# Turns of k between the output halves in pairs 0 to 2, and w2 loaded in thirds

## The chip, the cores and the metric

The kernel runs on one core of a Trainium2 chip. The metric is device time in microseconds (us) of one execution; lower is better. A core has a matrix engine (PE, whose weight loads are shown apart as PEld), a vector engine (DVE), a scalar engine (ACT), a general one (POOL) and SP, which here only issues the transfers (DMAs) from and to the memory outside the core. Each engine works through its own list in order; semaphores hold an instruction back until what it needs is there.

## The reference

A linear attention with decay in blocks, and after it a token-and-channel mixer:

```python
for b in range(nb):                       # 12 blocks of 64 positions
    intra = einsum('bhic,bhjc->bhij', qb, kb) * Dmask
    intra = einsum('bhij,bhjd->bhid', intra, vb)
    inter = einsum('bhid,bhde->bhie', qb * lam_pow, kv_state)
    out[:, :, sl] = intra + inter
    kv_state = lam_block * kv_state + einsum('bhsd,bhse->bhde', kb * rev_pow, vb)
x = out with heads joined                 # 4 x 768 x 512
h = relu(x^T @ w_tok1) @ w_tok2           # over the positions: 768 -> 256 -> 768
u = x + h^T
out = u + relu(u @ w_ch1) @ w_ch2         # over the channels: 512 -> 1536 -> 512
```

q, k, v are 4 x 8 x 768 x 64 in float32. The four weights come in 64-bit floats, read as pairs of 32-bit words.

## The kernel before

**Pairs.** The attention goes over 16 pairs i = 0..15 of two heads of one batch; blocks are 128 positions here, 6 to a pair. Names: `kn`, `qn`, `vn` are k, q, v as loaded; `kT`, `qT` their transposes; `sc` scores, `a` the scores with the decay mask; `kd` k with its decay; `kv` the sums of a block for the state, `sv` the states after the scan over the blocks, `stb` the states as the products need them; `qs` q with its decay; `xT` the outputs of half a pair (three blocks) in PSUM, copied by ACT to `uT`.

**Staging.** One turn of the loop (lines 556 to 619) holds work of three pairs. Turn i writes, in this order: the scores of pair i+1 (`scores`, PE L290, DVE L299) and `scale_q` (POOL L244); the first half of the outputs of pair i (`outputs(i, 0)`, PE L314 and L324, ACT L331); the state of pair i+1 (`state`, PE L257, scan on DVE L265); the second half `outputs(i, 1)`; for pair i+2 the mask scans (DVE L168, pairs 1 to 3 alone) and the turns: `turn_k` (PE L208, ACT L213) in pairs under 8, `turn_q_rows` (PE L228, ACT L229) in pairs under 5, from pair 5 a DVE transpose of q (L218); then `place` (POOL L278, `sv` to `stb`); then, in two halves, `turn_back` of pair i (PE L346 `xp`, ACT L354 `xhi`, DVE L355 `xlo`), with `scale_k` of pair i+2 (`kd`, ACT L237 and POOL L239) between; and last the loads of later pairs. From turn 4 groups of the mixer over positions (`token_hidden` L450, `token_out` L470) are put in.

**Order.** The schedule is by hand: each engine's list is the order in which the code is written.

**Buffers.** The tag "sh" has three PSUM banks, taken in turn by `kt`, `qt`, `kv`, `xp`, `ph`, `pu`; whoever takes a bank waits until the tile three places earlier has been read. `xT` has one bank, so the second half of the outputs waits for ACT's copy (L331) of the first. `kn` and `qn` have two buffers, `vn` three.

**Weights.** w1 comes in three loads (`load_w1`, 512 KB each) at turn -1, w2 in one of 1.5 MB (`load_w2`) at the end of turn 1. `convert_w1(i)` and `convert_w2(i)` put the steps of one third on the list `waiting`: ACT L379, DVE L380, L383, L386, L389, L392, then ACT L374 and POOL L375. `later(n)` writes the next n of them (n+1 where over five wait) between the steps of a turn, so a third that is put on the list at the end of turn i is worked through in turn i+1. In turns 1 to 3 that is w1; its L392 stands on DVE behind both `xlo`, and its L374 on ACT ahead of the next turn's L331.

**After the pairs.** From about 170 us on PE runs the mixer over channels (L645 `ph`, L666 `po`) nearly without a gap to the end.

Of the kernel before, what the change touches and what calls it, by code (L numbers as in the profile page):

```python
# [13 lines left out]
U32 = mybir.dt.uint32  # L14
# [7 lines left out]
def kernel(  # L22
# [23 lines left out]
    nc = tc.nc  # L46
    B, H, S, D = q.shape
# [3 lines left out]
    P = 128  # L51
# [3 lines left out]
    NK = FT // P  # L55
# [23 lines left out]
    def bank(tag, nm, n):  # L79
        return ps.tile([P, n], F32, tag=tag, bufs={"sc": 4, "xT": 1, "sh": 3}[tag], name=nm)  # L80
# [7 lines left out]
    NI = len(pairs)  # L88
# [5 lines left out]
    NKD = 8  # L94
# [71 lines left out]
    def masks(p):  # L166
        for h in (2 * p, 2 * p + 1):
            nc.vector.tensor_tensor_scan(  # L168
                out=mask[:, h],
                data0=lamb[:, h : h + 1].broadcast_to([P, P]),  # L170
                data1=ident,
                initial=0.0,
                op0=ALU.mult,
                op1=ALU.add,
            )
# [12 lines left out]
    n = 1  # L188
    while n < P:
        nc.vector.tensor_mul(  # L190
            out=lamp[:, :, n : 2 * n], in0=lamp[:, :, 0:n], in1=lamp[:, :, n - 1 : n].broadcast_to([P, NP, n])
        )
        n *= 2
    for p in range(NP):
        nc.gpsimd.tensor_copy(
            out=keep[:, p, :, 1:], in_=lamp[:, p, P - 1 : P, None].broadcast_to([P, D, NC - 2])
# [18 lines left out]
    def turn_q(i):  # L215
        qTs[i] = ap.tile([P, S], F32, tag="qT", bufs=2, name=f"qT{i}")
        if i >= NQ:
            nc.vector.transpose(out=qTs[i], in_=loaded[i][1])  # L218
        if i >= NKD:
            kTs[i] = ap.tile([P, S], F32, tag="kT", bufs=2, name=f"kT{i}")  # L220
            nc.vector.transpose(out=kTs[i], in_=krs[i])
# [19 lines left out]
    def scale_q(i):  # L241
        b, p = pairs[i]
        qss[i] = ap.tile([P, NC - 1, P], F32, tag="qs", bufs=2, name=f"qs{i}")
        nc.gpsimd.tensor_mul(  # L244
            out=qss[i],
            in0=qTs[i][:, P:].rearrange("p (c i) -> p c i", i=P),
            in1=lamp[:, p, None, :].broadcast_to([P, NC - 1, P]),
        )

    def state(i):  # L250

        b, p = pairs[i]
        kv = bank("sh", f"kv{i}", D * (NC - 1))
        to = kv.rearrange("p (e c) -> p c e", c=NC - 1)
        for c in range(NC - 1):
            for h in range(2):
                nc.tensor.matmul(  # L257
                    out=to[h * D : (h + 1) * D, c, :],
                    lhsT=kds[i][:, h, c, :],
                    rhs=vns[i][:, h, c, :],  # L260
                    start=(c == 0),
                    stop=(c == NC - 2),
                )
        sv = ap.tile([P, D * (NC - 1)], F32, tag="sv", bufs=1, name=f"sv{i}")
        nc.vector.tensor_tensor_scan(  # L265
            out=sv,
            data0=keep[:, p].rearrange("p e c -> p (e c)"),
            data1=kv,
            initial=0.0,
            op0=ALU.mult,  # L270
            op1=ALU.add,
        )
        st = stb[i % 2]

        def place():
            for h in range(2):
                r = slice(h * D, (h + 1) * D)
                nc.gpsimd.tensor_copy(out=st[r, :, h, :], in_=sv[r].rearrange("p (e c) -> p c e", c=NC - 1))  # L278

        return place  # L280

    def scores(i):
        b, p = pairs[i]
        for g in range(2):
            sc = [bank("sc", f"sc{i}{g}{h}", 3 * P) for h in range(2)]
            for c in range(3):
                cs = slice((3 * g + c) * P, (3 * g + c + 1) * P)
                for h in range(2):
                    r = slice(h * D, (h + 1) * D)
                    nc.tensor.matmul(  # L290
                        out=sc[h][:, c * P : (c + 1) * P],
                        lhsT=kTs[i][r, cs],
                        rhs=qTs[i][r, cs],
                        start=True,
                        stop=True,
                    )
            for h in range(2):
                a = ap.tile([P, 3, P], F32, tag="a", bufs=8, name=f"a{i}{g}{h}")
                nc.vector.tensor_mul(  # L299
                    out=a,  # L300
                    in0=sc[h].rearrange("p (c i) -> p c i", i=P),
                    in1=mask[:, 2 * p + h, None, :].broadcast_to([P, 3, P]),
                )
                weights_of[i, g, h] = a

    def outputs(i, g):
        b, p = pairs[i]
        st = stb[i % 2]
        xT = bank("xT", f"xT{i}{g}", 3 * P)
        for cg in range(3):  # L310
            c = 3 * g + cg
            cs = slice(cg * P, (cg + 1) * P)
            for h in range(2):
                nc.tensor.matmul(  # L314
                    out=xT[h * D : (h + 1) * D, cs],
                    lhsT=vns[i][:, h, c, :],
                    rhs=weights_of[i, g, h][:, cg, :],
                    start=(cg == 0),
                    stop=False,
                )  # L320
            if c == 0:
                continue
            for h in range(2):
                nc.tensor.matmul(  # L324
                    out=xT[h * D : (h + 1) * D, cs],
                    lhsT=st[:, c - 1, h, :],
                    rhs=qss[i][:, c - 1, :],
                    start=False,
                    stop=(cg == 2),
                )  # L330
        nc.scalar.copy(out=uT[b][:, p, 3 * g * P : (3 * g + 3) * P], in_=xT)  # L331
# [68 lines left out]
    def words(b):  # L400
        return uT[b].rearrange("p t s -> p (t s)").bitcast(U32)

    def load_w1(i):
        cs = slice(2 * i, 2 * i + 2)
        nc.sync.dma_start(
            out=words(3).rearrange("p (c f) -> p c f", c=NC)[:, cs],
            in_=w_tok1.bitcast(U32).rearrange("(c s) f -> s c f", s=P)[:, cs],
        )
# [8 lines left out]
            lambda x: x.rearrange("p (c f) -> p c f", f=FT),  # L417
        )

    def load_w2():  # L420
        nc.sync.dma_start(
            out=words(2).rearrange("p (k s) -> p k s", k=NK),
            in_=w_tok2.bitcast(U32).rearrange("(k f) s -> f k s", f=P),
        )

    def convert_w2(i):
        raw = words(2).rearrange("p (n two) -> p n two", two=2)
# [128 lines left out]
    for i in range(-2, NI):  # L556
        if 0 <= i + 1 < NI:
            scores(i + 1)
            scale_q(i + 1)
        if i >= 0:  # L560
            outputs(i, 0)
        place = state(i + 1) if 0 <= i + 1 < NI else None
        work = [groups.popleft() for _ in range(take.get(i, 0))]
        if i == NI - 1:
            work.pop(0)()
        if i >= 0:
            outputs(i, 1)
        if i + 2 < NI:
            turn_q(i + 2)
        if i + 2 < NI:  # L570
            if 0 < i + 2 < NP:
                masks(i + 2)
            turns = [(turn_k, 0), (turn_k, 1)] if i + 2 < NKD else []
            if i + 2 < NQ:
                turns += [(turn_q_rows, 0), (turn_q_rows, 1)]
            if i == -2:
                turns.sort(key=lambda x: x[1])
            for f, g in turns:
                f(i + 2, g)
        if place:  # L580
            place()
        later(1 if work else 2)
        n = early.get(i, len(work) // 4)
        cuts = [0, n, max(n, (3 * len(work) + 1) // 4 if len(work) > 2 else len(work) // 2), len(work)]
        for n in range(3):
            for f in work[cuts[n] : cuts[n + 1]]:
                f()
                later(2 if len(work) < 3 else 1)
            if n < 2 and i >= 0:
                turn_back(i, n)  # L590
                later(1 if work else 2 + n)
            if n == 0 and i + 2 < NI:
                scale_k(i + 2)
        if i == -1:
            load_w1(0)
        if 0 <= i + 3 < NI and i >= -1:
            load_v(i + 3)
        if i == -1:
            load_w1(1)
        if i + 4 < NI:  # L600
            load_kq(i + 4)
        if i == -1:
            load_w1(2)
        if i == 1:
            load_w2()
        if 0 <= i < 3:
            convert_w1(i)
        if 2 <= i < 4:
            convert_w2(i - 2)
        if i == 3:  # L610
            convert_w2(2)
        if i == 5:
            weights[0], load, convert = load_group(0, wa, early_scratch)
        if 5 <= i < 9:
            load(i - 5)
        if 6 <= i < 10:
            convert(i - 6)
        if i == 9:
            waiting.extend(split_block(0, up))
# [153 lines left out]
```

## Time and profile before

| what | value |
|---|---|
| median of 3 runs | 598.8 us (598.21 to 598.8) |
| profiled execution | 597.98 us, of which the span of the instructions is 596.2 us |
| PE busy | 577.9 us (97%) |
| DVE, ACT, POOL busy | 349.7, 155.2, 138.7 us |
| chain that ended last | PE 88%, DMA 4%, DVE 4%, ACT 2%, issue 1% |
| DMA busy | the first ten of 40 slices (149 us) at 9 tenths or more, one of them at 8; then 0 to 2 tenths until shortly before the end |

The span is the time from the first to the last instruction; what lies around it in the profiled execution is 1.78 us. PE is the engine on which nearly all of the time lies, so a stall counts where PE waits, and 18.3 us of the span are all that PE is not busy, start and end included. All of the pairs that the change touches lie in the first 60 us.

### The profile page before, as it was taken

How to read it: one execution, taken by the hardware profiler on the slowest of the kernel's cores; microseconds unless marked ns; L12 is line 12 of the kernel's file. 1: busy time of each engine (PE TensorE's matmuls, PEld its weight loads, DVE VectorE, ACT ScalarE, POOL GpSimd, SP SyncE). 2: the span in 40 equal slices, each digit the busy share in tenths (PEclk: the TensorE clock that was granted, in tenths of full speed). 3: DMA queues.
4: the chain of work that ended last, by engine and by line, in shares of the span. 5: the costliest groups of instructions: out<-in, count | busy, mean ns of one | idle time of the engine just before them, and what ended most of it. 6: DMA issues, size and time to landing. Idle time of an engine off the chain costs nothing.

```text
span 596.2 us, 10673 instructions
## 1 busy us (share of the span) xinstructions
PE 577.9 (97%) x4378; PEld 563.0 (94%) x4378; DVE 349.7 (59%) x663; ACT 155.2 (26%) x322; POOL 138.7 (23%) x131
## 2 busy tenths in 40 slices
PE   5988899999999999999999999999999999999997
PEld 4878798889999999999999999999999999999996
DVE  4797887886633666356533654356533664356664
ACT  3554434343232244112210221112210221101011
POOL 5665532462304367101100010001100010000000
PEclk9999999999999999999999999999999999999999
DMA  9998999999110111012100210012100200016667
GB/s 187 255 227 163 176 167 183 195 155 140 37 37 0 37 50 57 1 36 70 37 1 0 71 50 23 0 36 71 36 1 1 70 1 1 0 24 94 90 89 130
DMA packets 169680, 44.73 MB, mean 75 GB/s; under 512 B 162848, under 2 KB 164000, under 8 KB 169632
## 3 DMA queue, kind: packets, MB, share of 16 engines
q1 hardware_dynamic: 165488, 42.88, 37.4%
q10 hardware_dynamic: 4144, 1.18, 0.9%
q8 instruction: 34, 0.56, 0.4%
q14 instruction: 14, 0.11, 0.1%
HBM read 37.75 MB, written 6.29 MB: 74 GB/s over the span
## 4 chain that ended last, share of the span: by engine, by line
PE 88%; DMA 4%; DVE 4%; ACT 2%; issue 1%; SPq 0%; POOL 0%; DVEq 0%; ACTq 0%
PE ph L645 34%; PE po L666 34%; PE ph L450 6%; DMA kn<-in_k_dram 4%; PE pu L470 4%; PE xT L314 3%; PE sc L290 3%; PE xT L324 2%; PE xp L346 1%; PE kv L257 1%; DVE xlo L355 1%; DVE uT L389 1%; PE kt L208 1%; ACT qT L229 0%; PE qt L228 0%
## 5 line engine op out<-in xcount | busy, mean ns | idle before, releaser
L650 DVE SCALAR_TENSOR_TENSOR hl<-ph,hh 128x384 fp32r<-128x384 f32 x96 | 53.5, 558 | 164.9 <-ACT hh L649 164.9
L666 PE MATMUL po<-hh,c2h 128*128 128x384 f32 x384 | 129.4, 337 | 0.0
L645 PE MATMUL ph<-uh,c1h 128*128 128x384 f32 x384 | 129.2, 337 | 0.0
L645 PE MATMUL ph<-ul,c1h 128*128 128x384 f32 x384 | 129.2, 336 | 0.0
L645 PE MATMUL ph<-uh,c1l 128*128 128x384 f32 x384 | 129.1, 336 | 0.0
L666 PE MATMUL po<-hh,c2l 128*128 128x384 f32 x384 | 128.8, 335 | 0.0
L666 PE MATMUL po<-hl,c2h 128*128 128x384 f32 x384 | 128.6, 335 | 0.0
L649 ACT ACTIVATE hh<-ph 128x384 fp32r<-128x384 f32 x96 | 47.2, 492 | 299.6 <-PE ph L645 297.9
L671 DVE TENSOR_TENSOR uT<-po,uT 128x384 f32<-128x384 f32 x192 | 104.7, 552 | 23.5 <-PE po L666 23.4
L666 PEld LDWEIGHTS po<-hh,c2l 128*128 128x128 f32 x384 | 72.1, 188 | 0.0
L645 PEld LDWEIGHTS ph<-ul,c1h 128*128 128x128 f32 x384 | 72.1, 188 | 0.0
L666 PEld LDWEIGHTS po<-hl,c2h 128*128 128x128 f32 x384 | 72.1, 188 | 0.0
L645 PEld LDWEIGHTS ph<-uh,c1h 128*128 128x128 f32 x384 | 72.1, 188 | 0.0
L645 PEld LDWEIGHTS ph<-uh,c1l 128*128 128x128 f32 x384 | 72.1, 188 | 0.0
L666 PEld LDWEIGHTS po<-hh,c2h 128*128 128x128 f32 x384 | 72.0, 188 | 0.0
L375 POOL TENSOR_TENSOR c1l<-wa,c1h 128x512 fp32r<-128x512 f32 x10 | 12.9, 1290 | 179.9 <-ACT c1h L374 179.9
L535 POOL TENSOR_TENSOR ul<-uT,uh 128x384 fp32r<-128x384 f32 x32 | 36.0, 1154 | 37.5 <-ACT uh L534 37.5
L314 PE MATMUL xT<-a,vn 128*64 128x128 f32 x384 | 36.4, 280 | 1.9 <-ACT uT L331 1.9
L278 POOL COPY stb<-sv 64x320 f32<-64x320 f32 x32 | 26.4, 826 | 43.5 <-DVE sv L265 42.6
L299 DVE TENSOR_TENSOR a<-sc,mask 128x384 f32<-128x384 f32 x64 | 31.2, 550 | 5.7 <-PE sc L290 5.6
L324 PE MATMUL xT<-qs,stb 128*64 128x128 f32 x320 | 31.3, 273 | 0.0
L331 ACT COPY uT<-xT 128x384 f32<-128x384 f32 x32 | 15.3, 478 | 54.4 <-PE xT L324 54.4
(80 smaller groups left out, 758.1 us busy)
## 6 DMA issues: line engine op xcount, KB each, us to landing
raw<-in_moe_w_ch_dram SPq DMA_DIRECT2D x20, 512.0 KB, 3.6
vn<-in_v_dram SPq DMA_DIRECT2D x16, 384.0 KB, 5.5
kn<-in_k_dram SPq DMA_DIRECT2D x30, 192.0 KB, 5.3
out_dram<-y SPq DMA_DIRECT2D x108, 48.0 KB, 1.9
qn<-in_q_dram SPq DMA_DIRECT2D x44, 96.0 KB, 4.2
kr<-in_k_dram SPq DMA_DIRECT2D x32, 96.0 KB, 4.0
uT<-in_moe_w_ch_dram SPq DMA_DIRECT2D x4, 512.0 KB, 4.6
qn<-in_q_dram SPq DMA_DIRECT2D x8, 192.0 KB, 4.4
```

What stands on the lines that cost most here:

```text
L278: nc.gpsimd.tensor_copy(out=st[r, :, h, :], in_=sv[r].rearrange("p (e c) -> p c e", c=NC - 1))
L299: nc.vector.tensor_mul(out=a, in0=sc[h].rearrange("p (c i) -> p c i", i=P), in1=mask[:, 2 * p + h, None, :].broadcast_to([P, 3, P]),)
L314: nc.tensor.matmul(out=xT[h * D : (h + 1) * D, cs], lhsT=vns[i][:, h, c, :], rhs=weights_of[i, g, h][:, cg, :], start=(cg == 0), stop=False,)
L324: nc.tensor.matmul(out=xT[h * D : (h + 1) * D, cs], lhsT=st[:, c - 1, h, :], rhs=qss[i][:, c - 1, :], start=False, stop=(cg == 2),)
L450: nc.tensor.matmul(out=ph, lhsT=w[:, c, fs], rhs=x[:, c], start=(i == 0), stop=(i == 3 * NC - 1))
L470: nc.tensor.matmul(out=pu, lhsT=h[:, kk, cs], rhs=w[:, kk, ss], start=(i == 0), stop=(i == 3 * NK - 1))
L535: nc.gpsimd.tensor_sub(out=ul[:, t], in0=ub[:, t], in1=uh[:, t].bitcast(F32))
L645: nc.tensor.matmul(out=ph, lhsT=w[:, ct, js], rhs=x[:, ct], start=(i == 0), stop=(i == 11))
L649: nc.scalar.activation(hh, ph, AF.Relu)
L650: nc.vector.scalar_tensor_tensor(out=hl, in0=ph, scalar=0.0, in1=hh.bitcast(F32), op0=ALU.max, op1=ALU.subtract)
L666: nc.tensor.matmul(out=po, lhsT=w[:, jj, cs], rhs=h, start=(i == 0), stop=(i == 3 * JG - 1))
L671: nc.vector.tensor_add(out=ub, in0=po, in1=ub)
```

## The change

In turns 0, 1 and 2 the two `turn_k` of pair i+2 move from behind the second half of the outputs to between the halves, and the state of pair i+1 moves from between the halves to behind the second. The other turns are as before. The load of w2 becomes three: the first third in turn 1 ahead of pair 5's k and q, the second (in two pieces, since it crosses from one block of rows to the next) in turn 1 behind them, the last in turn 2 behind pair 5's v and ahead of pair 6's k and q.

```diff
-    def load_w2():
-        nc.sync.dma_start(
-            out=words(2).rearrange("p (k s) -> p k s", k=NK),
-            in_=w_tok2.bitcast(U32).rearrange("(k f) s -> f k s", f=P),
-        )
+    def load_w2(i):
+
+        n = 2 * NK * S // 3
+        k0, k1 = i * n // (2 * S), ((i + 1) * n - 1) // (2 * S)
+        for k in range(k0, k1 + 1):
+            ks = slice(max(i * n, 2 * S * k) - 2 * S * k, min((i + 1) * n, 2 * S * (k + 1)) - 2 * S * k)
+            nc.sync.dma_start(
+                out=words(2).rearrange("p (k s) -> p k s", k=NK)[:, k, ks],
+                in_=w_tok2.bitcast(U32)[k * P : (k + 1) * P, ks],
+            )
...
             outputs(i, 0)
-        place = state(i + 1) if 0 <= i + 1 < NI else None
+        turns = [(turn_k, 0), (turn_k, 1)] if 0 <= i < 3 else []
+        for f, g in turns:
+            f(i + 2, g)
+        place = state(i + 1) if 0 <= i + 1 < NI and not turns else None
...
             outputs(i, 1)
+        if turns:
+            place = state(i + 1)
         if i + 2 < NI:
             turn_q(i + 2)
...
-            turns = [(turn_k, 0), (turn_k, 1)] if i + 2 < NKD else []
+            turns = [(turn_k, 0), (turn_k, 1)] if not turns and i + 2 < NKD else []
...
+        if i in (1, 2):
+            load_w2({1: 0, 2: 2}[i])
         if i + 4 < NI:
             load_kq(i + 4)
...
         if i == 1:
-            load_w2()
+            load_w2(1)
```

PE in turn 1, from the end of the first half of the outputs of pair 1 (`xT_385`) to `turn_back`, before (`kn_236` is k of pair 3, `vn_233` v of pair 2):

```order
L324 MATMUL xT_385<-qs_267,stb_113 64x128 x2
L257 MATMUL kv_397<-vn_233,kd_342 64x64 x10
L314 MATMUL xT_410<-a_263,vn_107 64x128
...
L324 MATMUL xT_410<-qs_267,stb_113 64x128 x2
L208 MATMUL kt_428<-ident,kn_236 128x128 x3
L208 MATMUL kt_433<-ident,kn_236 128x128 x3
L228 MATMUL qt_438<-ident,qn_237 128x128 x3
L228 MATMUL qt_443<-ident,qn_237 128x128 x3
L346 MATMUL xp_453<-ident,uT_60 128x128 x3
```

and the same place now:

```order
L324 MATMUL xT_385<-qs_267,stb_113 64x128 x2
L208 MATMUL kt_398<-ident,kn_236 128x128 x3
L208 MATMUL kt_403<-ident,kn_236 128x128 x3
L314 MATMUL xT_408<-a_263,vn_107 64x128
...
L324 MATMUL xT_408<-qs_267,stb_113 64x128 x2
L257 MATMUL kv_422<-vn_233,kd_342 64x64 x10
L228 MATMUL qt_438<-ident,qn_237 128x128 x3
L228 MATMUL qt_443<-ident,qn_237 128x128 x3
L346 MATMUL xp_453<-ident,uT_60 128x128 x3
```

The turns of k come earlier by a half of the outputs, the sums `kv` later by that half and the turns. In the row of "sh" banks `kv` now stands three places ahead of the first `xp`. The order on DVE and on POOL does not change at all: the scan `sv` still stands directly behind the four `a` and ahead of the mask scans and of the conversion of w1.

ACT at the same place, as a difference:

```order
 L331 COPY uT_60<-xT_385 128x384
-L331 COPY uT_60<-xT_410 128x384
-L213 COPY kT_427<-kt_428 128x384
-L213 COPY kT_427<-kt_433 128x384
-L229 COPY qT_424<-qt_438 128x384
-L229 COPY qT_424<-qt_443 128x384
+L213 COPY kT_397<-kt_398 128x384
+L213 COPY kT_397<-kt_403 128x384
+L331 COPY uT_60<-xT_408 128x384
+L229 COPY qT_435<-qt_438 128x384
+L229 COPY qT_435<-qt_443 128x384
 L379 ACTIVATE uT_61<-uT_63 128x512
```

The two copies of `kT` now stand ahead of the copy of the second half; the steps of the conversion keep their place.

SP, the loads from pair 4's v (`vn_473`) to pair 6's k, before:

```order
L146 DMA vn_473<-in_v_dram 128x12x64
L126 DMA kn_475<-in_k_dram 128x6x64 x2
L104 DMA qn_476<-in_q_dram 32x24x32 x4
L421 DMA uT_62<-in_moe_w_tok_dram 128x2x1536
L146 DMA vn_598<-in_v_dram 128x12x64
L126 DMA kn_600<-in_k_dram 128x6x64 x2
```

and now (w2 is the one into `uT_62`):

```order
L146 DMA vn_473<-in_v_dram 128x12x64
L426 DMA uT_62<-in_moe_w_tok_dram 128x1024
L126 DMA kn_476<-in_k_dram 128x6x64 x2
L104 DMA qn_477<-in_q_dram 32x24x32 x4
L426 DMA uT_62<-in_moe_w_tok_dram 128x512 x2
L146 DMA vn_600<-in_v_dram 128x12x64
L426 DMA uT_62<-in_moe_w_tok_dram 128x1024
L126 DMA kn_603<-in_k_dram 128x6x64 x2
```

A third of w2 moves ahead of pair 5's k and q, and a third behind pair 5's v; pair 6's k still comes behind all of it, and SP issues three DMAs more.

## The prediction

> **What bounds the kernel now.** I read the page first, for who is busy, then the waits (us in total, times, longest), for what PE stands still on, then the stretches of the first 66 us (length, then busy time of PE, PEld, DVE, ACT, POOL, then the granted clock), where the change lies.
>
> ```profile
> span 596.2 us, 10673 instructions
> PE 577.9 (97%) x4378; PEld 563.0 (94%) x4378; DVE 349.7 (59%) x663; ACT 155.2 (26%) x322; POOL 138.7 (23%) x131
> ```
>
> ```profile
> PE xp L346 <- DVE sv L265: 2.2, 1, 2.2
> ...
> PE xT L314 <- ACT uT L331: 1.9, 2, 1.0
> ```
>
> ```profile
> 30.00:40.00 10.00, 9.10 (x148) 8.07 (x146) 9.17 (x17) 4.95 (x13) 6.03 (x5) 1.00 1.05 177
> 40.00:50.00 10.00, 7.58 (x120) 6.76 (x122) 9.90 (x19) 5.60 (x12) 8.03 (x7) 1.00 0.96 254
> ...
> 62.00:66.00 4.00, 1.79 (x16) 1.44 (x14) 4.00 (x7) 2.06 (x5) 0.79 (x1) 1.00 1.10 172
> ```
>
> PE is the bound over the whole, so only a longer or a shorter stall of PE counts. But from 30 to 50 us the third column of busy time, DVE, has 9.17 and 9.90 of 10 us, while PE stands still now and then: there DVE, busy with the pairs and with the conversion of w1, sets the pace. PE's list shows the places (start, time, then what; 23.85 to 28.42 is turn 1, the wait at 32.74 turn 2's, that at 41.00 turn 3's, the others turn 4's):
>
> ```profile
> 23.85 0.75 PE L257 MATMUL kv<-vn,kd 128*64 128x64 f32 x20
> 24.60 0.44 PE L314 MATMUL xT<-a,vn 128*64 128x128 f32 x4
> ...
> 26.06 0.87 PE L208 MATMUL kt<-ident,kn 128*128 128x128 f32 x6
> 26.78 0.95 PE L228 MATMUL qt<-ident,qn 128*128 128x128 f32 x6
> 27.56 0.93 PE L346 MATMUL xp<-ident,uT 128*128 128x128 f32 x6
> 28.42 1.61 PE L290 MATMUL sc<-qT,kT 64*128 64x128 f32 x24
> ...
> 31.10 0.75 PE L257 MATMUL kv<-vn,kd 128*64 128x64 f32 x20
> 32.74 0.44 PE L314 MATMUL xT<-a,vn 128*64 128x128 f32 x4 [0.89 <-ACT uT L331]
> ...
> 41.00 0.44 PE L314 MATMUL xT<-a,vn 128*64 128x128 f32 x4 [1.01 <-ACT uT L331]
> ...
> 48.33 0.80 PE L257 MATMUL kv<-vn,kd 128*64 128x64 f32 x20 [1.42 <-DMA vn<-in_v_dram]
> 48.93 0.42 PE L314 MATMUL xT<-a,vn 128*64 128x128 f32 x4
> ...
> 50.90 0.85 PE L208 MATMUL kt<-ident,kn 128*128 128x128 f32 x6 [0.46 <-DMA kn<-in_k_dram]
> ```
>
> The second halves of pairs 2 and 3 wait 0.89 and 1.01 us for ACT's copy of the first. The copy is late because of DVE:
>
> ```profile
> 24.72 0.82 DVE L265 TENSOR_TENSOR_SCAN sv<-keep,kv 128x320 f32<-128x320 f32 x1
> ...
> 26.62 0.93 DVE L380 TENSOR_SCALAR uT<-uT 128x512 uint32<-128x512 uint32 x1
> ...
> 29.24 0.56 DVE L355 TENSOR_TENSOR xlo<-xp,xhi 128x384 fp32r<-128x384 f32 x1 [0.76 <-ACT xhi L354]
> ...
> 30.98 0.68 DVE L392 SCALAR_TENSOR_TENSOR uT<-uT 128x512 uint32<-128x512 uint32 x1
> 31.58 1.95 DVE L299 TENSOR_TENSOR a<-sc,mask 128x384 f32<-128x384 f32 x4
> 33.44 0.81 DVE L265 TENSOR_TENSOR_SCAN sv<-keep,kv 128x320 f32<-128x320 f32 x1
> ...
> 37.39 0.56 DVE L355 TENSOR_TENSOR xlo<-xp,xhi 128x384 fp32r<-128x384 f32 x1 [0.73 <-ACT xhi L354]
> ...
> 39.24 0.68 DVE L392 SCALAR_TENSOR_TENSOR uT<-uT 128x512 uint32<-128x512 uint32 x1
> ...
> 43.30 0.42 DVE L380 TENSOR_SCALAR uT<-uT 128x512 uint32<-128x512 uint32 x1
> ```
>
> ```profile
> 31.70 0.62 ACT L374 CAST w1h<-uT 128x512 fp32r<-128x512 f32 x1 [1.66 <-DVE uT L392]
> 32.22 0.47 ACT L331 COPY uT<-xT 128x384 f32<-128x384 f32 x1
> ```
>
> From the scan at 24.72 on DVE goes through its list with one rest of 0.76 us up to L392; ACT's cast (31.70) waits for L392 (from 30.98), the copy (32.22) stands behind the cast, and PE goes on at 32.74. So PE's second half comes 1.76 us after the start of L392. In turn 3 it is the same: L392 at 39.24, PE at 41.00, again 1.76.
>
> **The change part by part.** Times are of the profiled execution.
>
> *Turn 0.* Turns of k (26.78 - 26.06 = 0.72 us in turn 1's rows) and sums (24.60 - 23.85 = 0.75) change places; no conversion waits behind the scan there. The first `xp` now waits for the scan, and meets it as it ends. I take nothing, between a loss of 0.2 (the wait) and a gain of 0.1.
>
> *Turn 1, the wait for k.* `turn_k` of pair 3 now stands where `kv` stood, at 23.85, in place of 26.06. The second half of that k is issued at 19.7 and lands 5.2 later:
>
> ```profile
> L126 SPq DMA_DIRECT2D kn<-in_k_dram x1: 950/950/950, 19.7 to 19.7; - x1
> ...
> DMA to landing us min/median/max: 5.2/5.2/5.2
> ```
>
> That is 24.9. Its place in SP's list is ahead of all that is changed, so it lands then again. With the 0.13 us or so from a landing to PE's first row, PE stands until 25.03, 1.18 us. Everything queued on PE behind it waits: the second half of the outputs, the sums, and with them DVE's scan. If k lands half a microsecond earlier or later, so does this term.
>
> *Turn 1, the late scan.* Turns 0.72, second half 26.06 - 24.60 = 1.46, sums to scan 24.72 - 23.85 = 0.87: the scan starts at 25.03 + 3.05 = 28.08 in place of 24.72, 3.36 us later, and DVE, whose four `a` are done by then, rests that long. Its list behind the scan is unchanged and packed, so L392 comes later by 3.36 less the one rest of 0.76, which is used up: **2.60**. PE's second half of pair 2 starts at 32.74 + 2.60 = 35.34. PE itself reaches it sooner: the first `xp` waits for the scan's end (28.90, three banks on from `kv`; the 2.2 us of the waits above are this kind of wait), `xp` takes 28.42 - 27.56 = 0.86, scores and first half 31.10 - 28.42 = 2.68, turns 0.72: 33.16. It stands 2.2 us in place of 0.89.
>
> *Turn 1 on POOL.* `place` and POOL's part of `kd` stand behind the scan too:
>
> ```profile
> 25.60 1.66 POOL L278 COPY stb<-sv 64x320 f32<-64x320 f32 x2 [2.88 <-DVE sv L265]
> 27.36 1.14 POOL L239 TENSOR_SCALAR kd<-kn,mask 128x320 f32<-128x320 f32 x1
> ```
>
> With 3.36 added `stb` is there at 30.62, and PE needs it after the scores of pair 3, which begin at 28.90 + 0.86 = 29.76 and take 1.61: 0.75 us to spare. `kd` of pair 3 ends at 31.86, its sums come after 36. SP's load of pair 5's k waits for that `kd`, some tenths, long before turn 3 uses it. All of this costs nothing.
>
> *Turn 2.* The second half (1.46) and the sums (0.87) put the scan at 37.67, 4.23 later than 33.44; DVE's four `a` came 2.60 later, so it rests 1.63. Less the rest of 0.73 at 37.39, L392 and the second half of pair 3 come **3.50** later: PE at 44.50 in place of 41.00. k of pair 4, issued last at 27.2, has landed at 31.9, and PE asks at 32.4, so nothing is lost there.
>
> ```profile
> L126 SPq DMA_DIRECT2D kn<-in_k_dram x1: 1036/1036/1036, 27.2 to 27.2; - x1
> ...
> DMA to landing us min/median/max: 4.7/4.7/4.7
> ```
>
> *Turn 3* is written as before, so DVE's list just runs 3.50 later, up to the cast and the copy of pair 4.
>
> *w2 in thirds.* Pair 5's v no longer comes behind all of w2, so it lands earlier by about a third of it, and the 1.42 us at 48.33 go. Alone that gives nearly nothing:
>
> ```profile
> 48.36 0.46 ACT L331 COPY uT<-xT 128x384 f32<-128x384 f32 x1
> ```
>
> The second half of pair 4 waits for this copy too, and 48.36 + 0.52 (32.74 - 32.22) = 48.88, against 48.93 now: 0.05 us. k of pair 6 still comes behind all of w2; it lands at about 50.8 as before, and PE now asks 3 us later, so the 0.46 us at 50.90 go, hidden behind what was lost. Pair 5's k and q come a third of w2 later; turn 3, which is 3.5 us late, does not feel it. The three added DMAs cost SP some 0.6 us each at the rate of such rows (0.95 and 1.04 above), on a queue that feeds nothing late: nothing, at most 0.5 us on pair 6's k, which has 3 us to spare.
>
> *The sum.* 2.60 + 0.90 - 0.05 - 0.46 = **+3.0 us** where turn 4's mixing starts. From there PE is the bound, with waits that hang on PE's own work, so the loss stays to the end. The profiled execution was 597.98, its span 596.2 and 1.78 around it; the median of the runs is 598.8. 598.8 + 3.0 = **601.8 us**.
>
> The most unsure term is DVE's time from the scan to L392. L380, the same step, took 0.93 us beside POOL and 0.42 (43.30) elsewhere. Since POOL's copies follow the scan as before, I keep 0.93; at 0.42 in both turns the loss is 1.0 us smaller, and if more of DVE's steps meet POOL, as much larger. With half a microsecond for k's landing the likeliest case reaches from +1.5 to +4.4: 600.3 to 603.2.
>
> **The rivals.**
>
> *DVE takes it.* DVE is 9.17 of 10 us busy, not 10, and the steps of w1 might be done in the wait for `kv`, so that nothing but the 1.18 us at k are lost, and the waits of 0.89 and 1.01 shrink by as much. Then PE is at 50.90 about when it was: 598.3 to 599.4, no change (0.2% of 598.8, or 1.2 us, is about what a measurement of this kernel tells from none). For it: turn 1's rows end in a rest. Against it: DVE's list is in order and the scan stands ahead of the conversion. Chance 0.11.
>
> *Faster.* Place: the state of pair 5 at 48.33. With w2 in thirds pair 5's v lands before PE asks, and the 1.42 and 0.46 us are saved, -1.88: 596.9. It decides if the copy at 48.36 comes over 1 us earlier too, that is, if turns 1 to 3 run faster on DVE than before; for that the turns of k between the halves would have to give ACT's copy the time that it now lacks, and the scan's delay would have to cost nothing. The sums gave it the same 0.75 us before. Chance 0.10.
>
> *The clock.* PE's longer stalls could lower its clock for a while. In its first microseconds the same scores took 2.27 us, later 1.61:
>
> ```profile
> 8.44 2.27 PE L290 MATMUL sc<-qT,kT 64*128 64x128 f32 x24
> ...
> 13.92 1.61 PE L290 MATMUL sc<-qT,kT 64*128 64x128 f32 x24 [0.24 <-ACT qT L229]
> ```
>
> One such stretch of 4 us costs 4 x (1 - 1.61/2.27) = 1.2 us, so 603.0. Against it: the stall of 2.2 us in 62 to 66 has a granted clock of 1.00 in its row, and the longest stall that I expect is as long. Chance 0.04, with the likeliest case's sign. [...]
>
> **How the numbers follow.** The likeliest, a late scan on DVE, has 0.75, and nearly all of it lies over 600.0; the clock 0.04 beside it; no change 0.11; faster 0.10. So faster 0.10, same 0.13 (a little of the first case's low end), slower 0.77. The predicted time is 601.8. The range must leave out no more than 2 in 10: it takes in the likeliest case, the clock and part of the case without change, 599.3 to 603.4.
>
> **What would show it.** Right: a wait of 0.9 to 1.3 us of `kt` on the load of k in turn 1; the scan of turn 1 near 28 us; the waits of the second halves on ACT's copy 2.2 and 1.7 us long; no wait on v at pair 5; `kt` of pair 6 near 53.9. Wrong: if `kt` in turn 1 does not wait, 1.18 of the 3.0 us go; if L392 of turn 1 still starts before 32, the case without change holds; if the conversion goes on beside a late scan, my reading of DVE as the pace there is wrong.

## The result, and the profile after

The changed kernel takes **603.05 us** (median of 3 runs, 601.71 to 603.41) against 598.8 (598.21 to 598.8): 1.0072 times the time before, 95% interval 1.0054 to 1.0089. It is slower, by 4.25 us; 3.0 was forecast, and the median lies inside the range. Executions of one kernel fall into groups by the mean clock that PE was granted (1.00 is full speed): the profiled execution before (0.998) shows no fall of the clock ahead of one at 593.54 us, that of e7 below (0.997) one and that after (0.993) two, so 0.998 or more is taken here for no fall, 0.995 to 0.997 for one and 0.993 or less for two, and times are set against each other at equal clock where the text says so.

The head of the profile's page after, with the granted clock in 40 slices:

```profile
span 601.2 us, 10675 instructions
PE 580.8 (97%) x4378; PEld 565.7 (94%) x4378; DVE 349.6 (58%) x663; ACT 155.6 (26%) x322; POOL 139.2 (23%) x131
...
PEclk9989899999999999999999999999999999999999
```

PE does the same 4378 matmuls, in a span that is 5.0 us longer. The waits after (us in total, times, longest) are those that the prediction named:

```profile
PE kt L208 <- DMA kn<-in_k_dram: 6.7, 4, 5.2
...
PE xT L314 <- ACT uT L331: 3.9, 3, 1.7
...
PE xp L346 <- DVE sv L265: 2.6, 3, 2.2
```

ACT's copy now holds PE for 3.9 us instead of 1.9. PE's list after, turns 1 to 4 (start, time, work, and the idle time ahead of it with its releaser):

```profile
25.12 0.85 PE L208 MATMUL kt<-ident,kn 128*128 128x128 f32 x6 [0.95 <-DMA kn<-in_k_dram]
...
27.26 0.75 PE L257 MATMUL kv<-vn,kd 128*64 128x64 f32 x20
...
29.00 0.88 PE L346 MATMUL xp<-ident,uT 128*128 128x128 f32 x6 [0.19 <-DVE sv L265]
...
32.78 0.85 PE L208 MATMUL kt<-ident,kn 128*128 128x128 f32 x6
35.31 0.44 PE L314 MATMUL xT<-a,vn 128*64 128x128 f32 x4 [1.68 <-ACT uT L331]
...
45.11 0.44 PE L314 MATMUL xT<-a,vn 128*64 128x128 f32 x4 [1.00 <-ACT uT L331]
...
52.98 0.44 PE L314 MATMUL xT<-a,vn 128*64 128x128 f32 x4 [1.22 <-ACT uT L331]
...
54.44 0.87 PE L208 MATMUL kt<-ident,kn 128*128 128x128 f32 x6
```

In turn 1 PE stands 0.95 us for pair 3's k, and in turn 2 1.68 us for the copy of pair 2's first half. The last row stood at 50.90 before: 3.54 us later. The scores of pair 7, further on, begin at 75.36 in place of 70.30, so 1.5 us more are lost between the two. DVE in turns 1 and 2:

```profile
28.13 0.82 DVE L265 TENSOR_TENSOR_SCAN sv<-keep,kv 128x320 f32<-128x320 f32 x1 [3.27 <-PE kv L257]
...
30.04 0.93 DVE L380 TENSOR_SCALAR uT<-uT 128x512 uint32<-128x512 uint32 x1
...
33.55 0.68 DVE L392 SCALAR_TENSOR_TENSOR uT<-uT 128x512 uint32<-128x512 uint32 x1
...
39.60 0.40 DVE L380 TENSOR_SCALAR uT<-uT 128x512 uint32<-128x512 uint32 x1
```

DVE rests 3.27 us ahead of the scan and then works through the same list as before. What the prediction had not counted stands in two pairs of stretches (length; busy time of PE, PEld, DVE, ACT, POOL; then the granted clock):

```profile
32.42:35.83 3.41, 1.60 (x22) 1.16 (x18) 3.38 (x8) 1.57 (x4) 0.87 (x1) 1.00 1.00 239
35.83:39.25 3.42, 3.42 (x43) 3.30 (x39) 0.65 (x2) 0.67 (x2) 1.91 (x2) 0.50 1.12 213
...
66.56:69.97 3.41, 1.23 (x11) 1.23 (x12) 3.13 (x7) 1.71 (x5) 1.16 (x2) 1.00 1.14 160
69.97:73.38 3.41, 3.41 (x19) 3.41 (x18) 1.20 (x4) 1.47 (x4) 2.88 (x3) 0.50 1.32 173
```

Twice a stretch with little work on PE (1.60 and 1.23 of 3.41 us) is followed by 3.41 us at a granted clock of 0.50. The first fall comes behind the stall of 1.68 us in turn 2, the second behind a stall of 2.20 us in turn 5 that stands in the kernel before as well (2.21 us), and there no fall came behind it in its profiled execution.

### The profile page after: what moved, and what is told of

Its sections match the earlier page's. It is cut to its first block, busy times and chain, and to the rows that moved or that the text cites. A ratio compares the mean times of both kernels' runs of the same rounds, so it can differ in the third digit from the quotient of the medians.

```text
span 601.2 us, 10675 instructions
## 1 busy us (share of the span) xinstructions
PE 580.8 (97%) x4378; PEld 565.7 (94%) x4378; DVE 349.6 (58%) x663; ACT 155.6 (26%) x322; POOL 139.2 (23%) x131
## 3 DMA queue, kind: packets, MB, share of 16 engines
q10 hardware_dynamic: 4144, 1.18, 0.9%
## 4 chain that ended last, share of the span: by engine, by line
PE 84%; DVE 5%; DMA 4%; SPq 3%; POOL 1%; issue 1%; ACT 1%; ACTq 0%; DVEq 0%; POOLq 0%
PE ph L657 34%; PE po L678 33%; PE ph L455 5%; PE pu L475 4%; DMA qn<-in_q_dram 3%; PE xT L314 2%; PE sc L290 2%; SPq L104 2%; PE xT L324 2%; PE xp L346 1%; SPq L126 1%; DMA kn<-in_k_dram 1%; PE kv L257 1%; DMA vn<-in_v_dram 1%; DVE uT L480 1%
## 5 line engine op out<-in xcount | busy, mean ns | idle before, releaser
L314 PEld LDWEIGHTS xT<-a,vn 128*64 128x64 f32 x384 | 22.5, 137 | 8.0 <-ACT uT L331 4.6
```

Source lines behind the costliest of these rows:

```text
L314: nc.tensor.matmul(out=xT[h * D : (h + 1) * D, cs], lhsT=vns[i][:, h, c, :], rhs=weights_of[i, g, h][:, cg, :], start=(cg == 0), stop=False,)
```

## The experiments

**One half of the change at a time.** e1 is the kernel before with w2 in thirds alone:

```diff
+        if i in (1, 2):
+            load_w2({1: 0, 2: 2}[i])
         if i + 4 < NI:
             load_kq(i + 4)
...
-            load_w2()
+            load_w2(1)
```

> Only w2 is loaded in thirds; the loop's order is that of before. Theory 'late scan' (the change costs 3 us because PE waits for pair 3's k and, above all, because the scan of the states reaches DVE over 3 us late): no scan is late here, so no loss; pair 5's v lands before PE asks (the wait of 1.42 us goes), but the copy of pair 4's first half still holds PE to about 48.9 and pair 6's k to about 50.9: 598.2 to 599.3, no change. Rival 'w2' (the smaller loads on SP are what costs, since more DMAs stand ahead of k and q): slower by 2 us or more. Rival 'faster' of the prediction: 596.9.

Measured: 598.81 us (597.58 to 600.25, 12 runs), 1.0009 [0.9997, 1.0021]. PE's list of e1 in turn 4:

```profile
48.77 0.44 PE L314 MATMUL xT<-a,vn 128*64 128x128 f32 x4 [1.05 <-ACT uT L331]
...
51.02 0.85 PE L208 MATMUL kt<-ident,kn 128*128 128x128 f32 x6 [0.72 <-DMA kn<-in_k_dram]
```

The wait for pair 5's v is gone, and the second half waits 1.05 us for ACT's copy instead, as the prediction worked out; k of pair 6 still comes last. Over all runs there is no gain, and no loss that the interval tells from none. At a clock of 0.998 or more, though, the median of e1's nine runs is 598.62 us and that of the 13 of the kernel before 597.71, so alone the thirds may cost some 0.9 us. In e1's trace q of pair 6 comes late: DVE turns it at 53.85 in place of 52.69, and PE then waits 1.14 us for pair 6's `kd` in place of 0.47:

```profile
60.86 0.74 PE L257 MATMUL kv<-vn,kd 128*64 128x64 f32 x17 [1.14 <-POOL kd L239]
```

That the thirds make this q late is not shown, since with w2 in one load it is turned at 51.79 (e8) or 53.47 (e3) too.

e2 is the changed kernel with w2 in one transfer, so the new order alone:

```diff
-        if i in (1, 2):
-            load_w2({1: 0, 2: 2}[i])
...
-            load_w2(1)
+            load_w2()
```

> Only the order in turns 0 to 2 is changed; w2 is one load as before. Late scan: the whole loss is here, +3.0 us on before (601.5 to 602.0) where the clock stays up, and 1 to 1.5 us more in an execution for each time that the clock falls; the scan of turn 1 starts at 28.1 and PE resumes pair 2's second half at 35.3. Rival 'w2': 598.8. Rival 'late k' (only PE's wait for pair 3's k costs, DVE takes the rest): +1.0.

Measured: 601.52 us (599.83 to 603.09, 6 runs), 1.0054 [1.0037, 1.0072]; scan of turn 1 at 27.99. The order alone has the whole loss (the changed kernel again, e7 below, has a ratio of 1.0044).

**The two halves of the order.** e3, on the kernel before, puts the turns of k between the halves and leaves the state ahead of the second half; e4 puts the state behind it and leaves the turns where they were:

```diff
         place = state(i + 1) if 0 <= i + 1 < NI else None
+        early_k = 0 <= i < 3
+        if early_k:
+            turn_k(i + 2, 0)
+            turn_k(i + 2, 1)
...
-            turns = [(turn_k, 0), (turn_k, 1)] if i + 2 < NKD else []
+            turns = [(turn_k, 0), (turn_k, 1)] if i + 2 < NKD and not early_k else []
```

```diff
-        place = state(i + 1) if 0 <= i + 1 < NI else None
+        behind = 0 <= i < 3
+        place = state(i + 1) if 0 <= i + 1 < NI and not behind else None
...
             outputs(i, 1)
+        if behind:
+            place = state(i + 1)
```

> On the kernel before: the turns of k stand between the halves in turns 0 to 2, but behind the state, which keeps its place; w2 as before. Late scan: the scan starts at 24.7 again, so nearly all of the loss goes although the turns of k are moved; turn 1 waits about 0.4 us for pair 3's k, turn 2 covers about 0.7 of the 0.89 us wait for ACT's copy; pair 5's v and pair 6's k then hold PE as before: 598.2 to 599.3, no change. Rival 'late k': the wait for k stays and costs its 0.4 us and what follows from it, 599.2 to 600. A theory by which the turns between the halves cost by themselves: +3.

> On the kernel before: the state stands behind the second half in turns 0 to 2, the turns of k behind it, where they were; w2 as before. PE does not ask for pair 3's k early. Late scan: the scan of turn 1 starts at 26.2 (+1.46), L392 and PE's second half of pair 2 come 0.7 later, those of pair 3 1.6 later; with the 0.5 us of pair 6's k used up +1.0 to +1.2 us: 599.8 to 600.0. Late k: no wait for k, so 598.8.

Measured: e3 599.45 us (598.97 to 600.22, 11 runs), 1.0017 [1.0006, 1.0029], just over what was expected; e4 601.13 (600.27 to 602.35, 6 runs), 1.0043 [1.0026, 1.0059]. All of e3's runs had the clock at 0.995 to 0.997, and runs of the kernel before at that clock took 599.03 to 600.41: at equal clock e3 loses nothing. Why its clock fell in every run is open. e3's scan and its wait for k:

```profile
24.56 0.82 DVE L265 TENSOR_TENSOR_SCAN sv<-keep,kv 128x320 f32<-128x320 f32 x1
```

```profile
25.04 0.85 PE L208 MATMUL kt<-ident,kn 128*128 128x128 f32 x6 [0.59 <-DMA kn<-in_k_dram]
```

k is late here too, but the scan has started by then, and the wait for k takes the place of the one for the copy. In e4 the scan is late (27.95), although PE waits for no k ahead of it. PE's list of e4, turns 0 to 2:

```profile
17.54 0.44 PE L314 MATMUL xT<-a,vn 128*64 128x128 f32 x4 [0.58 <-ACT uT L331]
...
25.72 0.44 PE L314 MATMUL xT<-a,vn 128*64 128x128 f32 x4 [0.58 <-ACT uT L331]
...
35.13 0.44 PE L314 MATMUL xT<-a,vn 128*64 128x128 f32 x4 [1.80 <-ACT uT L331]
```

I had expected less than was measured for e4: with nothing between the halves, each second half waits 0.58 us for ACT's copy, which the turns of k cover in the changed kernel and the sums did before. So the state behind the second half is enough for the loss, and the turns of k alone (e3) cost nothing at equal clock; in the changed kernel the turns of k decide what PE waits for ahead of the sums. The two delays are not made of the same parts: in e4 the waits for the copy, one of them in turn 0, stand where the changed kernel has the turns and the late k, so e4's time is no measure of the state's share in it.

**The late k.** e5 is the changed kernel with pair 3's k and q loaded ahead of the second third of w1:

```diff
-        if i == -1:
-            load_w1(1)
...
         if i + 4 < NI:
             load_kq(i + 4)
         if i == -1:
+            load_w1(1)
             load_w1(2)
```

> The full change, but pair 3's k and q are loaded ahead of w1's second and third third. Late scan: PE's wait of 0.95 us for k in turn 1 goes, and the scan of turn 1 starts at about 27.2 in place of 28.1; DVE's rest of 0.76 us in that turn stays used up, so the whole 0.95 us is won to the end and no more: 0.7 to 1.1 us under the changed kernel on the same chip, still 1.5 us or more over the kernel before. Late k: all of the loss goes, 598.

Measured: 601.14 us (600.64 to 602.69, 6 runs), 1.0051 [1.0035, 1.0067]. At a clock of 0.995 to 0.997 its runs took 600.64 to 601.18, the changed kernel's (e7, below) 601.55 to 601.93: 0.8 us won (the medians of these runs, 600.89 and 601.67). The wait in turn 1 is gone and the scan starts at 27.15; the next k is then late:

```profile
32.70 0.85 PE L208 MATMUL kt<-ident,kn 128*128 128x128 f32 x6 [1.02 <-DMA kn<-in_k_dram]
34.34 0.44 PE L314 MATMUL xT<-a,vn 128*64 128x128 f32 x4 [0.78 <-ACT uT L331]
```

**The clock.** e6 is the changed kernel with PE's two long stalls filled: the turns of k of pair 4 are done three times and those of pair 7 four times, each time with the same values.

```diff
-        for c in range(3):
+        for c in list(range(3)) * {4: 3, 7: 4}.get(i, 1):
```

> The full change; turn_k of pair 4 does its transposes 3 times and that of pair 7 4 times, into the same place, so that PE works in the stalls of turn 2 (1.7 us) and turn 5 (2.2 us) in place of standing; the result of the turns is the same. Theory 'clock' (of the loss, 1.5 to 2 us come from stretches of 3.4 us at half clock, which follow a window of 3.4 us in which PE stood for 1.7 us or more): no such stretch in any execution before the end, clock 0.997 or more in each, times all within about 0.6 us of each other and 1 to 3 us under the median of the changed kernel. If the clock's falls do not hang on the stalls: spread as the changed kernel's, and up to 0.5 us slower than it for the added work.

e7 is the changed kernel as it is, on the same chip:

> The changed kernel again, to have its times and clocks beside those of the others on one chip. Late scan with clock: times in groups by the granted clock, about 600.3 (0.998 or more), 602 (0.995 to 0.997), 603.3 (0.993 or less); the order alone was 599.8, 601.5 and 603.1 in these.

Measured: e6 600.35 us (600.22 to 600.82, 6 runs), 1.0032 [1.002, 1.0044], with the clock at 0.998 or more in every run; e7 601.55 (600.1 to 601.93, 7 runs), 1.0044 [1.0029, 1.0058], of which the three runs at 1.00 took 600.1, 600.1 and 600.57 and the others, at 0.995 to 0.997, 601.55 to 601.93. More work on PE made the median 1.2 us lower. PE's list of e6 shows the two stalls that are left:

```profile
35.32 0.44 PE L314 MATMUL xT<-a,vn 128*64 128x128 f32 x4 [0.54 <-ACT uT L331]
...
67.25 0.55 PE L346 MATMUL xp<-ident,uT 128*128 128x128 f32 x3 [0.23 <-DVE sv L265]
```

Pair 2's second half starts at 35.32, in e7 at 35.28, and e6's times are those of e7's runs at 1.00: the filling moves nothing, and the gain is the clock's. The kernel before, at 0.998 or more on this chip, took 597.17 to 598.09: without a fall the change costs some 2.35 us (600.1 less 597.75, the medians of these runs).

**DVE's list.** e9 is the changed kernel with the steps of w1's conversion put ahead of the state, so that DVE does them in its rest before the scan:

```diff
+        ahead = bool(turns)
+        if ahead:
+            later(2)
         place = state(i + 1) if 0 <= i + 1 < NI and not turns else None
...
-        later(1 if work else 2)
+        if not ahead:
+            later(1 if work else 2)
```

> The full change; in turns 0 to 2 the next steps of w1's conversion (ACT L379, DVE L380 and L383) stand ahead of the state, so that DVE does them while it waits for the late sums. PE's order, the wait for k and the late scan stay. Late scan (the scan costs because DVE's later work queues behind it): the scan of turn 1 still starts at about 28.1, but L392 starts near 32.2 in place of 33.5, PE resumes pair 2's second half near 34 in place of 35.3 and pair 3's 1 to 1.5 us earlier than in the changed kernel; 1.0 to 1.9 us of the 2.5 are won at the same clock: 598.3 to 599.2 where the changed kernel has 600.1 to 600.6. If the late scan costs by itself (its states, not the queue behind it): no better than the changed kernel.

Measured: 600.03 us (599.32 to 601.11, 7 runs), 1.0033 [1.0021, 1.0045]; at a clock of 0.998 or more 599.32 to 600.03. Against the kernel before at such a clock on the same chip (597.91, the medians of these runs) that is 1.6 us, where e7 had 2.35 on its own: some 0.75 us won, less than expected. DVE's list of e9:

```profile
28.12 0.82 DVE L265 TENSOR_TENSOR_SCAN sv<-keep,kv 128x320 f32<-128x320 f32 x1 [1.75 <-PE kv L257]
...
32.05 0.68 DVE L392 SCALAR_TENSOR_TENSOR uT<-uT 128x512 uint32<-128x512 uint32 x1
...
35.06 1.93 DVE L383 SCALAR_TENSOR_TENSOR uT<-uT,uT 128x512 uint32<-128x512 uint32 x1
```

With the scan as late as after (28.12 and 28.13) L392 comes 1.5 us earlier, and PE begins pair 3's second half at 42.59 (e7: 43.58). So a part of what the late scan costs, about a third, lies in the conversion that stood behind it. What is left was not taken apart by a run of its own; the trace shows that the next step (L383, 35.06) took 1.93 us, where it took 1.15 us in turn 2 after (40.03), and that PE then waits 0.83 us for turn 2's scan and 0.43 us for pair 6's k.

**The same order elsewhere.** e8 leaves turns 0 to 2 as before and uses the new order in turn 5 alone, where PE stood 2.2 us at `xp` for the scan:

```diff
-        place = state(i + 1) if 0 <= i + 1 < NI else None
+        early_k = i == 5
+        if early_k:
+            turn_k(i + 2, 0)
+            turn_k(i + 2, 1)
+        place = state(i + 1) if 0 <= i + 1 < NI and not early_k else None
...
+        if early_k:
+            place = state(i + 1)
```

> On the kernel before: the changed order in turn 5 alone, where neither kernel has it (pair 7's turns of k between the halves, pair 6's state behind). There DVE is 2 us behind PE, so that the scan cannot start before 64.3 however early its sums come. Late scan: the late sums cost nothing there, and since 'kv' then stands two banks later, the first 'xp' takes the bank of a 'kt' and no longer waits 2.2 us for the scan: 1.5 to 2.2 us faster, and the stall is gone that lowers the clock in some executions: 595.5 to 596.5, all in one group. A theory by which the order costs wherever it stands: slower by 0.5 us or more.

Measured: **596.21 us** (596.09 to 596.56, 5 runs), 0.9964 [0.9951, 0.9978], with the clock at 0.998 or more in every run. At such a clock the kernel before took 597.75 here, so 1.5 us come from the order and the rest from falls of the clock that e8 does not have. PE's list of the kernel before and then of e8 in turn 5:

```profile
60.08 0.74 PE L257 MATMUL kv<-vn,kd 128*64 128x64 f32 x17 [0.47 <-POOL kd L239]
...
62.12 0.87 PE L208 MATMUL kt<-ident,kn 128*128 128x128 f32 x6
65.20 0.55 PE L346 MATMUL xp<-ident,uT 128*128 128x128 f32 x3 [2.21 <-DVE sv L265]
```

```profile
59.07 0.87 PE L208 MATMUL kt<-ident,kn 128*128 128x128 f32 x6
...
61.24 0.75 PE L257 MATMUL kv<-vn,kd 128*64 128x64 f32 x20
61.92 0.55 PE L346 MATMUL xp<-ident,uT 128*128 128x128 f32 x3
...
64.93 0.52 PE L346 MATMUL xp<-ident,uT 128*128 128x128 f32 x3 [0.31 <-DVE sv L265]
...
66.15 0.38 PE L450 MATMUL ph<-xhi,w1h 128*128 128x256 f32 x1 [0.70 <-DVE xlo L355]
```

Here DVE was busy until the scan anyway: in the kernel before it starts at 64.34, 3.5 us after its sums are done (60.08 + 0.74); in e8 at 63.97. So the sums may come later at no cost. With the turns of k ahead of `kv`, `kv` and `xp` stand closer in the row of banks, the first `xp` and its products run ahead of the scan, and the 2.21 us shrink to 0.31 and 0.70.

**All together.** e10 has e9's steps in turns 0 to 2, e5's loads and e8's turn 5:

```diff
-        turns = [(turn_k, 0), (turn_k, 1)] if 0 <= i < 3 else []
+        turns = [(turn_k, 0), (turn_k, 1)] if 0 <= i < 3 or i == 5 else []
...
+        ahead = bool(turns) and i < 3
```

> As the kernel with the steps ahead, and pair 3's k loaded ahead of w1's second third, and the changed order in turn 5 too. Late scan: what is left of the loss in turns 0 to 2 is 0 to 0.8 us, and turn 5 wins its 2 us: 595.5 to 597.0, without a clock's fall. If the order in turns 0 to 2 has an advantage of its own that the scan hid: under 595.5.

Measured: 597.75 us (597.21 to 600.3, 12 runs), 0.9995 [0.9984, 1.0006]: no change to before, and worse than e8, which was not expected. In the profiled execution the loads hold PE in turns 2 to 4, as PE's list of e10 has it:

```profile
33.23 0.85 PE L208 MATMUL kt<-ident,kn 128*128 128x128 f32 x6 [1.07 <-DMA kn<-in_k_dram]
...
49.12 0.80 PE L257 MATMUL kv<-vn,kd 128*64 128x64 f32 x20 [1.15 <-DMA vn<-in_v_dram]
...
52.56 0.85 PE L208 MATMUL kt<-ident,kn 128*128 128x128 f32 x6 [1.08 <-DMA kn<-in_k_dram]
```

That execution took 600.3 us, the slowest of the twelve, at a mean clock of 0.997; how much of these waits the others have, and so what e10 lost against e8, is open.

## Why the prediction was right, and where it was not

**Turn 0** costs 0.25 us where nothing was put down: from the first products of pair 0 to the scores of pair 2 it lasts 5.96 us (15.36 to 21.32) in place of 5.71 (15.46 to 21.17). Of that, 0.19 us are the wait of the first `xp` for the scan, which had been allowed for with up to 0.2.

**Turn 1** went step by step as worked out: PE waits 0.95 us for k (1.18 forecast), the scan starts at 28.13 (28.08), L392 at 33.55 (33.58 by the sum's 2.60), PE's second half of pair 2 at 35.31 (35.34). Only the wait that the trace shows there is 1.68 and not 2.2 us, since PE came to it half a microsecond later than I had it. e5 gives the share of the late k, 0.8 us; e4 shows that the scan can be as late without it; e9 that some 0.75 us of the loss hang on the order of DVE's list.

**Turn 2 was mis-sized.** I had L392 3.50 us later, which keeps L380 at the 1.30 us of the kernel before (the 0.93 that I named is turn 1's row). In e7, where the clock stayed up until there, the scan stands where it was forecast (37.51 against 37.67), but not what follows it. DVE of the kernel before, then of e7:

```profile
34.16 1.30 DVE L380 TENSOR_SCALAR uT<-uT 128x512 uint32<-128x512 uint32 x1
```

```profile
37.51 0.82 DVE L265 TENSOR_TENSOR_SCAN sv<-keep,kv 128x320 f32<-128x320 f32 x1 [1.45 <-PE kv L257]
38.24 0.40 DVE L380 TENSOR_SCALAR uT<-uT 128x512 uint32<-128x512 uint32 x1
...
41.82 0.68 DVE L392 SCALAR_TENSOR_TENSOR uT<-uT 128x512 uint32<-128x512 uint32 x1
```

and POOL of the kernel before, then of e7:

```profile
33.63 1.54 POOL L244 TENSOR_TENSOR qs<-qT,lamp 128x640 f32<-128x640 f32 x1
```

```profile
36.17 1.56 POOL L244 TENSOR_TENSOR qs<-qT,lamp 128x640 f32<-128x640 f32 x1
```

Before, POOL's `qs` ran beside L380; now it is done when L380 starts, and L380 takes 0.40 us. L392 comes 2.58 us later than before (41.82 against 39.24) and not 3.50, so this term was 0.9 us too large. The prediction had named L380 as the unsure step and put 1.0 us on it for both turns; it came in turn 2 alone. Pair 6's first turn of k then stands at 52.91 in e7, 2.0 us later than before, where +3.0 was forecast.

**The clock was the step that failed.** I gave it 0.04 and held that a stall of 2.2 us passes, since the one at 62 to 66 showed 1.00. In the kernel before, that stall lies in two of the stretches that one gets by counting in steps of 3.41 us, the length of each fall after, back from its one fall, at 593.54 (155 steps to 64.47):

```profile
61.06:64.47 3.41, 1.94 (x27) 1.53 (x23) 3.38 (x7) 1.85 (x4) 0.48 (x1) 1.00 1.07 197
64.47:67.88 3.41, 2.68 (x23) 2.68 (x24) 2.44 (x4) 1.51 (x3) 2.53 (x3) 1.00 0.99 139
```

So the border at 64.47 cuts the stall into 1.47 and 0.73 us (3.41 less PE's 1.94 and 2.68). After the change PE stands still for 2.18 us of the 3.41 us ahead of the fall at 69.97, the whole stall in one stretch. That this is why the one passed and the other did not is my estimate from these two traces; no run shows such a border by itself. The first fall put pair 6's turn of k at 54.44 in place of e7's 52.91, 1.5 us, and the second took the 1.5 us between there and pair 7. Of the three runs of the changed kernel, two had a clock that goes with two falls (0.993 and 0.992) and one that of a single fall (0.997). That makes 2.0 us of mechanism and up to 3.0 of clock in the profiled execution, against 3.0 and none in the forecast. The two errors have opposite signs, so the sum is nearer than its terms: that the median lies so near the forecast is in part luck. By e7's 2.35 us at equal clock, my estimate is that some 1.9 of the 4.25 us are the clock's. The price that I gave one fall, 1.2 us for a stretch of 4 us that no row shows, was near: the two falls after lasted 3.41 us each and cost 1.5.

**w2 in thirds** did what was said with the rest: no wait for pair 5's v, none for pair 6's k, and ACT's copy in place of them (1.22 us at 52.98). Alone (e1) it took away the wait for v, and may cost 0.9 us.

**The rivals.** That DVE would take it fell with L392 at 33.55; the faster case fell with e1, and with the copy that comes later, not earlier. e8 shows that the order can make the kernel faster, in a turn that the change left as it was.

## What to carry to other kernels

The one instruction whose input came late held up all that stood behind it on its engine (in turn 1 DVE's scan came 3.41 us later than before, 28.13 against 24.72, and L392, further down the list, 2.57 us later, 33.55 against 30.98): before moving that input's producer back, look at what stands behind the consumer, and either move that ahead (e9) or move the producer where the consumer is late for its own reasons (e8, 1.5 us faster than the kernel before at equal clock). What stands between a half and the copy that frees its buffer is cover, and taking it away lays the wait for the copy open (0.58 us a turn in e4). A profile that shows no fall of the clock behind a stall does not clear that stall: the 2.21 us in turn 5 had none behind them in the profiled execution before, and the same stall had one after and in e7 (2.20 us each). So before adding a stall of two microseconds to PE, put the price of a fall, 1.5 us here, beside the gain, and read the clock of several executions.

## What the runs showed of the hardware

In the trace after, the granted clock is 0.50 from 35.83 to 39.25 and from 69.97 to 73.38, and again from 599.03; between these changes lie 3.41, 30.72, 3.41 and 525.65 us, which are 1, 9, 1 and 154 times 3.41. In the trace before it is 0.50 from 593.54 on alone.

The stalls ahead of the falls do not tell by their length alone whether one comes. In turn 5 PE stood 2.20 us after and in e7, and a fall came behind both (in e7 the rows of L455 take 0.41 us from 67.86 to 70.84, and 0.28 from 71.71 on); before it stood 2.21 us, with none. In turn 2 a fall came behind 1.68 us after, where the `kv` that follows takes 1.29 us; behind 1.83 us in e7 and 1.80 in e4 that `kv` takes 0.75. What decides was not shown; that it is how the stall lies in steps of 3.41 us is my estimate.

A fall cost 1.5 us there: from the `xp` that waits in turn 5 to the scores of pair 7 it is 6.62 us after and 6.61 in e7, with a fall, and 5.10 before, without. That agrees with the groups of e7's runs, whose medians lie 1.6 us apart (600.1 and 601.67).

In turn 2, L380 took 0.40 us after and in e7 (39.60 and 38.24), where POOL's `stb` began 0.14 and 0.15 us behind its start. It took 0.93 us in turn 1 both before and after, where a row of `stb` was running as it began and ended 0.64 us into it, and 1.30 us in turn 2 before, where `qs` was running and ended 1.01 us into it; L380 ended 0.29 us later each time. No run here shows the cause.
